# A fused attention and Fourier-mixing kernel: zero-tile dummy matmuls, half-wise table arguments, two-row folds and a new instruction order in the opening

## The chip, the cores and the metric

The kernel runs on one core of a Trainium2 chip. The metric is the device time of one execution in microseconds, as the median of several runs; less is better. The core has five engines with queues of their own: TensorE (PE in the profile, with its weight loads as PEld), VectorE (DVE), ScalarE (ACT), GpSimd (POOL) and SyncE (SP), which here only starts transfers.

## The reference

Cut to what matters. The inputs are x (8 batches, 8 heads, 512 rows, 64 columns), state (8, 8, 32, 64) and two weight matrices of 512 x 2048 and 2048 x 512, all in float32.

```python
scores = x @ state.T / sqrt(64);   a  = softmax(scores);   xread = a @ state
scores2 = state @ x.T / sqrt(64);  a2 = softmax(scores2);  sread = a2 @ x
z = concat([xread, sread], rows)              # per batch 544 rows x 512 columns (8 heads x 64)
mixed = real(fft(fft(z, rows), columns))
u = z + mixed
un = (u - mean(u)) / sqrt(var(u) + 1e-6)      # over the 512 columns
out = u + relu(un @ w_ch1) @ w_ch2
```

## The kernel before

The kernel works batch by batch. For each batch it makes the attention (scores, exponentials, two reads), folds the 544 rows and 512 columns by the symmetries of the Fourier transform, multiplies by cosine and sine tables along the rows (psum tiles `gp`) and along the columns (`yp`), adds the result to z (tile `U`), centres it (`ub`), transposes it (`tp`, `unT`), and runs the two layers: `ph` is a psum tile of the first layer, `hT` its result, `po` (batch 0) and `poA`, `poB` (later batches, in a Strassen form) those of the second. Weights live in `w1` and `w2` in bf16; eight transfers started by GpSimd bring and convert them, a quarter of a matrix each (`first_weights`, `second_weights`).

Nothing is scheduled by a compiler. Every operation is first recorded as a group (class `Recorder`, lines 21 to 64; `_Engine.__getattr__` makes the record), and `play` then issues the groups in the order of the list `ORDER`. So each engine's queue, and each transfer queue, follows that list. `BANKS` says which of six psum banks each tile gets. Consecutive matmuls into the same tile and bank form one group and cannot be separated. All operations have one line in the profile, L62, so they are told apart by their tiles.

Batch 0 has an opening of its own (`open_batch`, and the list from line 1261), because nothing else can run beside it:

- Loads. `load_x(0)` fills `xs` in seven pieces, four large (parts 0 to 3 of 128 rows; part 3 has 96 and three small pieces) and three small; `load_state(0, 1)` brings the state of batch 0 into `gen`. Two parts (2 and 0) go through ScalarE's queue, the others and the state through SP's.
- Tables. GpSimd makes integer ramps with iota (`pi_`, `gen`). `turn` makes from them the arguments of cosine and sine on VectorE, in four steps: counts, rests, products, ends. It makes two halves, [0] for the rows of x and [1] for the low rows (state rows and a few others). ScalarE turns them into the tables TC and TS; `minus` makes NC and NS, their negatives (tile NN). TEO is the table of the second axis.
- Attention. `cast_x` casts xs to bf16 (`xin`), `state_blocks` puts the state into a block form (`stb`), `turn_state` and `turn` transpose both on TensorE (tiles `warm` and `xTp`, copied to `sT` and `xT`), `score` multiplies them (`esp`), ScalarE takes exponentials (`EE`), `read` and `sread` form the reads (`xrp`, `warm`), and VectorE divides by the sums into XF, XR and XQ.
- Folds. `even(k)` and `odd(k)`, for k = 1 and 0, add and subtract reversed halves: Sm, then XE0 and XO0 (both in the memory of SS), and a column of ZB (in NN).
- Transform. `begin`, `low_of` (low rows, tables [1]) and `terms_of` (folds, tables [0]) accumulate four `gp` tiles; `out_of` copies them to G.
- Dummies. `warm(n)` records n matmuls of the identity tile `ident` with itself into a psum tile that nobody reads; `ORDER` spreads them over the opening (46 in all, 11 of them first).
- ScalarE loads a table of functions when it changes between exponentials and sines.

Batch 1 is loaded and cast meanwhile. GpSimd's `gate` operations make it wait for a chosen tile before it starts weight transfers: one on XO0, one on w1's last quarter, ahead of w2.

Of the kernel before, what the change touches and what calls it, by code (L numbers as in the profile page):

```python
# [20 lines left out]
class Recorder:  # L21
# [4 lines left out]
    def __init__(self, nc):  # L26
        self.nc, self.groups = nc, []
        for name in self.ENGINES:
            setattr(self, name, _Engine(self, name, getattr(nc, name)))
# [20 lines left out]
class _Engine:  # L50
# [3 lines left out]
    def __getattr__(self, what):  # L54
        f = getattr(self._engine, what)
        if not callable(f):
            return f

        def call(*args, **kw):
            out = kw.get("out", args[0] if args else None)  # L60
            key = (out.tensor.name, out.offset // 512 % 2) if self._name == "tensor" else None
            self._rec.add(self._name, lambda: f(*args, **kw), key)  # L62

        return call
# [3 lines left out]
        17 21 23 22 19 24 66 27-28 34 30 26 32 36 31 35 33 25 37 1 4 0 6 8 2 7 5 3 9 11 58 10 12 305 13-14 59 57 16 15 18 20 29  # L68
        42 40 39 38 41 86 89 43-46 49 48 47 51-52 50 53 55 54 80-82 96-97 87 90 56 98 109 111 93 113 112 110 83-85 94 114 124
        116 118 88 120 132 92 231 78 104 77 63 207 76 79 230 64 205 65 103 62 101 100 99 117 125 133 68 70 67 72-73 71 69 74 249  # L70
        75 95 115 134 136 135 137 146 153 147 91 122 138-139 154 140 155 108 141 229 144 206 142-143 201 106 149 126 148 150 128
        127 129 157 159 163 166 119 121 160-162 167 175 130 151 131 123 152 189 170 191 171-173 190 185 192 174 184 193 186
        197-199 158 169 165 156 178 180 168 216 179 164 182-183 196 194 187 209 188 212 176 181 195 177 211 217 214 210 213 107
        200 202-204 237 208 145 105 232 235 234 236 233 251 250 252 242 244 243 245 248 246-247 262 218 215 219 221 256 220
        223-226 253 222 227 260 259 255 254 257 261 258 271 273 451 272 274 315 263 269 277 275 270 278 281 283 267 265 328 264
        282 284 329 285 290-291 268 292-293 286 308 311-312 316 318 239 294 296-297 240 347 238 352 295 298-299 60 354 241 102
        320-321 313 309 314 310 322-323 371 279 306 330-331 326 317 287 319 266 327 307 402 372 332-333 453 334-336 338 454 337
        339 452 379 375-376 340 343 435 344 342 345 341 455 61 300 303 301 351 304 456 353 348-350 356 324 288 389 383 395 385
        369 387 393 406 391 403 399 397 390 325 289 276 521 396 280 386 384 388 394 370 392 400 398 418 404 410 448 381 411-412
        380 417 414 421-422 377 415 426 405 407-408 373 378 425 430-431 436 359-360 358 357 382 423 416 409 413 459 466 427 446  # L80
        428 419 447 432 429 420 508-509 437 433 504 457 434 401 438 302 506 510 458 505 346 507 363 362 365 367 364 361 366 473
        512 442 462 449 460 424 513 444 374 450 461 480 463 469 467 519 439 470 468 490-493 440 485 474 486 475 441 368 476 479
        702 477 483 478 489 482 487 484 514 488 528 522 464 515-516 560 552 530 494 499 497 531 536 544 517-518 523 532-533 503
        498 502 500-501 537-538 526 525 527 524 539-540 551 541 543 542 546-547 555 548 557 556 550 549 534 471 554 562 567 529
        465 481 561 545 535 520 553 568 472 582 607 563 571 569 565 495 564 572 570 566 576 591 598 558 496 583 592 608 577 579
        601 584 578 585 600 593 599 594 614 619 615 620 610 612 580 574 589 602 559 613 588 611 597 581 618 623 575 603 590
        644-645 681 634 666-667 687 691 646-647 631 586 630 670 629 228 628 648 658 657 659 587 660 663 662 661 511 604-605
        624-625 609 697 692 712 638 704-705 698 852 675 674 635 701 672 699 671 676 673 668 682 669 684 686 636 693-694 688 685
        683 706-707 639 708 713 709-710 721 716 720 724-725 717 719 718 632-633 606 643 726 627 695 748 742 794 714 722 732 727
        734 746 744 801 689 738 649 750 696 743 795 749 723 733 715 728 745 735 747 690 739 751 760 753 641 655 650 640 755 656  # L90
        642 637 652 736 740 803 729 758 664 810 767 653 651 756 754 757 665 730 711 731 677-678 779 792 772 761 802 737 804 759
        811 766 765 776 780 768 770 769 771 741 793 775 773 782 800 654 703 700 781 680 774 796 788 786 805 841 762 823 807 814
        812 822 763 813 806 787 626 783 789 797 817-818 849 834 816 832 837 904 838 819-820 842 833 851 595-596 821 752 826 621
        777 825 778 829 828 827 830-831 622 616 573 617 884 862 844 808 839-840 850 824 885 858-859 864 898 764 890 887 889 855
        853-854 809 1032 871-872 900 910 926 893 847 906 835 965 921 917 869 899 905 927 976 911 863 836 966 894 848 922 870 860
        843 861 865 873 846 845 867 874-878 868 901 895 879 896 916 880 907 918 897 883 882 881 908 914 923 1033 857 866 888 903
        856 892 891 886 977 919 912 937 915 924 909 920 913 938 978 933 928 942 970 939 983 952 954 988 1031 930 929 931 944 935
        943 934 932 971 936 984 940 955 941 990 1016 991 981 997 1007-1008 979 992 945-946 993 953 989 948 957 982 994 1000 798
        1001 1003-1004 1002 790 799 791 784 1005-1006 785 1009-1010 980 1017 1070 947 956 961 972 1210 1035 1034 1037 445 1064
        1069 1067-1068 1036 1012 967 1027-1028 985 1049 1076 1014 1166 1042 999 995 986 1013 1029-1030 996 1018 968 1021 1043  # L100
        1062 1038 1078 1024 1143 1096 1094 1040 1050 949 958 1077 1167 1063 1044 1019-1020 1045-1046 1048 1047 1056 1052 1025
        1011 1051 1054 1053 1071 1026 1073 1072 1060 1055 1041 1074 1088 1135 1084 1022 1123 1092 1098 1057 1090 1079 962 1015
        1144 1095 973 1039 1089 1097 1085 1136 1023 1124 1099 1075 1061 1058 1091 1093 1104 1161 1137 1118 1149 1080 1105-1107
        1081 1108 987 969 1066 1065 443 1109 1162 1150 1111-1112 1110 1209 925 950-951 355 959 1168-1169 1113 1102 1155 1086
        1194 1121 1159 1156 1087 1122 1160 1115 1138 1103 1101 1116 1119 1170 1114 1171 1120 1117 1173 1131 1126 1154 1127
        1211-1212 1059 998 1083 1130 1215 1125 1213-1214 1139 1145 1185 1175 1186 1190 1157 1218 1187-1188 1174 1158 1177 1204
        1191 1128 960 1172 974 1178 1180 1184 1179 1100 1183 1129 975 963-964 1205-1206 1151 1163 1265 1202 1207 1152 1219 1189
        1195 1234 1203 1208 1238 1198 1235 1200 1220-1221 1245 1182 1181 1197 1246 1222 1196 1164 1216 1251 1261 1227 1294 1273
        1249 1257 1267 1306 1240 1337 1192 1223 1199 1224 1226 1236 1225 1252 1242 1244 1262 1274 1229 1243 1230 1233 1231 1239
        1272 1291 1232 1201 1132 1140 1217 1266 1228 1250 1258 1146 1307 1295 1325 1338 1241 1268 1263 1255 1269 1289 1259 1270  # L110
        1264 1256 1260 1247 1284 1332 1320 1290 1248 1321 1333 1193 1328 1308 1365 1339-1340 1275 1287 1286 1285 1288 1309 1341
        1329 1342 1278 1276-1277 1279 1297 1302 1282 1298 1283 1237 1253 1165 1153 1316 1310 1296 1301 1343 1349 1351 1141-1142
        1350 1147 1354-1355 1133-1134 1148 1271 1353 1352 1299-1300 1322 1334 1356-1357 1346 1330 1292 1376-1377 1326 1314 1280
        1358 1366 1359 1370 1323 1335 1293 1303 1327 1281 1315 1331 1384-1385 1411 1421 1361 1371 1404 1391 1466 1380 1422 1412
        1405 1392 1381 1369 1368 1348 1378-1379 1386-1387 1398 1367 1388 1390 1389 1393 1406 1408 1394 1344-1345 1362 1375
# [53 lines left out]
def kernel(  # L169
# [30 lines left out]
    ctx.enter_context(tc.manual_schedule(engines={ET_.PE, ET_.DVE, ET_.Activation, ET_.Pool, ET_.SP}))  # L200


    ident = singles.tile([128, 128], BF16, name="ident")
    epst = singles.tile([128, 1], F32, name="epst")
    mhalf = singles.tile([128, 1], F32, name="mhalf")
    halfpi = singles.tile([128, 1], F32, name="halfpi")
# [1335 lines left out]
```

## Time and profile before

| what | us |
|---|---|
| runs (three) | 288.33, 288.52, 290.14; median 288.52 |
| profiled execution | 289.02 |
| its span, first to last instruction | 287.2 |
| TensorE busy | 275.9 (96%) |
| VectorE, ScalarE, GpSimd busy | 211.1, 161.7, 93.3 |
| first matmul | 4.32 |
| first matmul of the first layer (ph) | 23.43 |
| first matmul of the second layer (po) | 40.76 |
| granted TensorE clock (mean) | 0.995 |

All times inside the execution count from the start of the span; 1.8 us of the profiled execution lie outside of it. A line of the timeline gives start, busy time, engine, operation with its tiles and shapes, and in brackets the idle time before it with what ended it. A matmul's busy time includes the way through the array, so the distance between starts tells the rate. The granted clock of the profile's rows reads 1.00 from the start; whether TensorE runs at half or full rate is read from the distances of matmuls.

### The profile page before, as it was taken

What the parts mean: (1) busy time and instruction counts of PE and PEld (TensorE: products, weight loads), DVE (VectorE), ACT (ScalarE), POOL (GpSimd) and SP (SyncE); (2) the same over time, 40 slices, a digit from 0 to 9 for tenths busy, and PEclk for the clock granted to TensorE, in tenths of its full rate; (3) what the DMA queues carried; (4) which work ended last, traced back from release to release, by engine and by line L of the source; (5) the groups of instructions that cost most, each with busy time, mean ns of one, the idle gap of its engine ahead of it and who ended that gap; (6) DMA issues with size and microseconds to landing.
All of it is one profiled execution on the core that took longest, in us unless ns stands there. A gap on an engine that the chain in (4) does not pass through costs nothing.

```text
span 287.2 us, 6784 instructions
## 1 busy us (share of the span) xinstructions
PE 275.9 (96%) x2607; PEld 198.1 (69%) x2607; DVE 211.1 (74%) x557; ACT 161.7 (56%) x323; POOL 93.3 (32%) x227
## 2 busy tenths in 40 slices
PE   3999999999999999999999999999999999999992
PEld 2988985555655778566758777576577667687882
DVE  7688776468899988975798688959766578225882
ACT  5978584745936476368377564586566653254000
POOL 7673772570660043502812128006200028000000
PEclk9999999999999999999999999999999999999998
DMA  8999999966376237561398640313201520968466
GB/s 164 179 159 152 183 173 170 194 150 134 102 167 123 66 93 167 113 170 23 85 165 190 141 99 21 92 57 73 75 0 40 161 59 21 179 134 147 107 156 178
DMA packets 110972, 34.91 MB, mean 122 GB/s; under 512 B 101996, under 2 KB 106476, under 8 KB 110940
## 3 DMA queue, kind: packets, MB, share of 16 engines
q1 hardware_dynamic: 100220, 28.72, 48.5%
q0 software_dynamic: 4224, 4.19, 9.6%
q10 hardware_dynamic: 6496, 1.57, 2.5%
q8 instruction: 20, 0.33, 0.5%
q14 instruction: 12, 0.10, 0.1%
HBM read 22.41 MB, written 14.02 MB: 127 GB/s over the span
## 4 chain that ended last, share of the span: by engine, by line
PE 92%; DVE 4%; ACT 1%; issue 1%; POOL 0%; POOLq 0%
PE ph L62 41%; PE poA L62 18%; PE poB L62 13%; PE po L62 5%; PE gp L62 4%; PE yp L62 3%; PE esp L62 2%; PE xrp L62 1%; PE eTp L62 1%; PE xfp L62 1%; PE warm L62 1%; DVE gen L62 1%; DVE ot L62 1%; PE srp L62 1%; PE tp L62 1%
## 5 line engine op out<-in xcount | busy, mean ns | idle before, releaser
L62 PE MATMUL ph<-unT,w 128*128 128x512 bf16 (+2 forms) x768 | 129.6, 317 | 0.6 <-issue 0.5
L62 ACT ACTIVATE hT<-ph 128x512 bf16<-128x512 f32 x128 | 72.1, 596 | 77.6 <-PE ph L62 77.5
L62 PEld LDWEIGHTS <-w 128*128 128x128 bf16 x768 | 64.1, 98 | 42.9 <-issue 1.1
L62 PEld LDWEIGHTS <-hT 128*128 128x128 bf16 x632 | 60.5, 98 | 14.7 <-issue 0.3
L62 DVE SCALAR_TENSOR_TENSOR ot<-poA,rstd,U 128x256 f32<-128x256 f32 (+1 forms) x46 | 21.7, 475 | 16.5 <-PE poA L62 13.9
L62 POOL CAST xin<-xs 128x2048 bf16<-128x2048 f32 (+3 forms) x14 | 14.6, 1060 | 44.2 <-DMA xs<-in_x_dram 44.0
L62 PE MATMUL poB<-w,hT 128*128 128x256 bf16 x224 | 28.2, 273 | 0.0
L62 POOL TENSOR_TENSOR rstd<-rstd,mhalf 128x1 f32<-128x1 f32 x34 | 20.4, 608 | 1.1
L62 POOL TENSOR_TENSOR rstd<-mv,epst 128x1 f32<-128x1 f32 x14 | 2.5, 190 | 42.0 <-DVE mv L62 42.0
L62 ACT ACTIVATE ub<-U,S 128x512 bf16<-128x512 f32 (+1 forms) x22 | 15.1, 707 | 1.5 <-DVE U L62 1.3
L62 PE MATMUL po<-w,hT 128*128 128x512 bf16 x64 | 15.6, 379 | 0.0
L62 PE MATMUL poA<-TA,SB 128*128 128x256 bf16 x120 | 15.6, 273 | 0.0
L62 PE MATMUL poB<-TA,SA 128*128 128x256 bf16 x120 | 15.5, 272 | 0.0
L62 ACT CAST G<-gp 128x288 bf16<-128x288 f32 (+2 forms) x31 | 13.2, 481 | 4.0 <-PE gp L62 3.8
L62 DVE SCALAR_TENSOR_TENSOR U<-yp,XF 128x2 f32<-128x2 f32 (+1 forms) x24 | 10.0, 418 | 7.5 <-PE yp L62 5.3
L62 DVE SCALAR_TENSOR_TENSOR ot<-poB,rstd,ot 128x256 f32<-128x256 f32 x30 | 14.2, 477 | 1.0 <-PE poB L62 0.9
L62 PE MATMUL poA<-TC,hT 128*128 128x256 bf16 (+1 forms) x120 | 14.5, 265 | 0.1
L62 PE MATMUL poA<-w,hT 128*128 128x256 bf16 x112 | 14.5, 273 | 0.0
L62 ACT ACTIVATE junk<-U,S 128x512 bf16<-128x512 f32 x20 | 14.3, 716 | 0.2
L62 PE MATMUL poA<-TB,hT 128*128 128x256 bf16 x112 | 14.3, 272 | 0.0
L62 DVE SCALAR_TENSOR_TENSOR ot<-poB,rstd,U 128x256 f32<-128x256 f32 x15 | 7.2, 478 | 9.0 <-PE poB L62 9.0
L62 POOL COPY XT<-XR 32x514 bf16<-32x514 bf16 x7 | 4.2, 605 | 27.6 <-DVE U L62 16.5
(195 smaller groups left out, 475.6 us busy)
## 6 DMA issues: line engine op xcount, KB each, us to landing
xs<-in_x_dram SPq DMA_DIRECT2D x22, 256.0 KB, 3.9
w<-in_moe_w_ch_dram POOLq DMA_DIRECT2D x8, 512.0 KB, 6.6
out_dram<-ot SPq DMA_DIRECT2D x15, 256.0 KB, 2.4
r_dram<-ot SPq DMA_DIRECT2D x14, 256.0 KB, 2.3
out_dram<-r_dram SPq DMA_DIRECT2D x14, 256.0 KB, 3.7
xs<-in_x_dram SPq DMA_DIRECT2D x8, 192.0 KB, 3.7
xs<-in_x_dram ACTq DMA_DIRECT2D x2, 256.0 KB, 4.4
l_dram<-ot SPq DMA_DIRECT2D x2, 256.0 KB, 2.0
```

The source lines that it names most:

```text
L62: self._rec.add(self._name, lambda: f(*args, **kw), key)
```

## The change

1. A tile `blank` of zeros is set by VectorE at the start. `warm` multiplies it with itself, instead of `ident`. The first call records 48 dummies instead of 11. In the recorder, a matmul whose two operands are the same tile now is a group of its own, so the order can place each dummy by itself; 44 stand at the head of TensorE's queue, 83 are issued in all.
2. `turn` gives its four steps for each half. Half 0 is made at the start; `low_arguments` makes half 1 later. The sines and the negations are issued per half (288 wide instead of 576); those of half 1, and all negations, come after the exponentials of batch 0.
3. `even` and `odd` work on both rows k at once (1028 wide instead of 514, and so on).
4. The eight first loads form one group (`held`), issued in a fixed sequence. Within SP's queue part 1 now goes ahead of part 3. ScalarE casts three of four state blocks ahead of part 2 of x.
5. GpSimd makes the ramps of the x rows ahead of other constants.
6. `ORDER` and `BANKS` are new. What the new order does to the queues, read from the built programs:
   - VectorE casts part 0, copies the first transposed part, casts part 1, copies the state, casts part 3; half 1 of the arguments stands between the copies of xT and the reciprocals of batch 0.
   - GpSimd casts one part of x of batch 1, starts the first quarter of w1, does its part of XB, NN and stb, then starts the other three quarters of w1 together; after casts of batch 1 it starts w2's first quarter, after the copy of XR of batch 1 (XT) the second, after a root's first addition the last two. The gate on w1's last quarter now stands behind w2's transfers.
   - SP issues the loads of x of batch 1 in another order, and four pieces of x of batch 2 between the two transposes of the state of batch 2 that stood together before.
   - TensorE takes the sixteen steps of batch 0's first layer in another order; the quarter of w1 that arrives first is read first, and the last quarter is read from the tenth step on instead of the fifth. The first `gp` of batch 1 comes after fourteen steps instead of sixteen.
   - From about 44 us on, all engines' instructions stand in the same order in both kernels.

The diff, without the numbers of the order and the banks:

```diff
-            key = (out.tensor.name, out.offset // 512 % 2) if self._name == "tensor" else None
+            product = self._name == "tensor" and ("lhsT" not in kw or kw["lhsT"] is not kw["rhs"])
+            key = self._rec.held or ((out.tensor.name, out.offset // 512 % 2) if product else None)
...
+    blank = singles.tile([128, 128], BF16, name="blank")
+    nc.vector.memset(blank, 0.0)
...
-            for queue, n in ((nc.sync, None), (nc.scalar, 2), (nc.sync, 3), (nc.scalar, 0), (nc.sync, 4), (nc.sync, 5), (nc.sync, 6),
-                             (nc.sync, 1)):
+            nc.held = "first loads"
+            for queue, n in ((nc.scalar, 2), (nc.scalar, 0), (nc.sync, None), (nc.sync, 4), (nc.sync, 6), (nc.sync, 5), (nc.sync, 1),
+                             (nc.sync, 3)):
...
+            nc.held = None
...
-        def rests():
-            nc.vector.tensor_scalar(q2d, in0=q2d, scalar1=float(1 << 23), scalar2=-float(N), op0=ALU.subtract, op1=ALU.mult)
+        def rests(i):
+            nc.vector.tensor_scalar(q[:, i, :], in0=q[:, i, :], scalar1=float(1 << 23), scalar2=-float(N), op0=ALU.subtract, op1=ALU.mult)
...
+    def low_arguments():
+        nc.vector.tensor_copy(lo_, pi_[:, 2:3])
...
+        for step in turn_steps:
+            step(1)
...
-        nc.scalar.activation(TC, q1, AF.Sin, bias=halfpi, scale=-w_rows)
+    def sine_c(i):
+        nc.scalar.activation(TC[:, i], q1[:, i], AF.Sin, bias=halfpi, scale=-w_rows)
...
-        def even(k):
-            nc.vector.tensor_add(Sm[:, k], XF[:, k], XR[:, k])
+        def even():
+            nc.vector.tensor_add(Sm, XF, XR)
...
-            nc.tensor.matmul(warmed["tile"][:, 0:128], lhsT=ident, rhs=ident, start=True, stop=True)
+            nc.tensor.matmul(warmed["tile"][:, 0:128], lhsT=blank, rhs=blank, start=True, stop=True)
...
-    turn_products()
-    turn_ends()
-    sine_s()
-    sine_c()
+    sine_s(0)
+    sine_c(0)
     exp_again()
-    warm(11)
+    warm(48)
...
     exp2()
+    low_arguments()
...
-    minus(NC, TC)
-    minus(NS, TS)
+    minus(NC[:, 0], TC[:, 0])
+    minus(NS[:, 0], TS[:, 0])
     sin_table()
+    sine_s(1)
+    sine_c(1)
...
-    even(1)
+    even()
     second_sines()
     second_halves()
+    minus(NC[:, 1], TC[:, 1])
+    minus(NS[:, 1], TS[:, 1])
...
-    odd(1)
+    odd()
     terms_of(2, 1), terms_of(3, 1)
-    even(0)
...
-    odd(0)
```

## The prediction

> **What bounds the kernel now.** I read the chain of waits first. It gives TensorE nearly everything, so a change pays only if TensorE's main stream starts sooner.
>
> ```profile
> PE 92%; DVE 4%; ACT 1%; issue 1%; POOL 0%; POOLq 0%
> ```
>
> Then TensorE's waits, longest first. After its first instruction it is starved for about 1.5 us in the whole span; the one long wait is at the start, where the dummies wait for the identity tile that GpSimd makes.
>
> ```profile
> PE warm L62 <- POOL ident L62: 4.3, 1, 4.3
> PE tp L62 <- ACT ub L62: 0.5, 1, 0.5
> PE ph L62 <- issue: 0.5, 1, 0.5
> ```
>
> "Never starved" is not "full speed". The timeline of TensorE (start, busy us, operation) shows what the busy share hides:
>
> ```profile
> 4.32 1.35 PE L62 MATMUL warm<-ident 128*128 128x128 bf16 x11 [4.32 <-POOL ident L62]
> 8.32 0.58 PE L62 MATMUL esp<-xT,sT 128*128 128x128 bf16 x4
> ...
> 9.99 0.61 PE L62 MATMUL esp<-xT,sT 128*128 128x128 bf16 x4
> ...
> 11.71 0.83 PE L62 MATMUL warm<-ident 128*128 128x128 bf16 x12
> ...
> 17.98 0.23 PE L62 MATMUL gp<-NN,SS 128*128 128x144 bf16 x1
> ...
> 22.45 0.40 PE L62 MATMUL tp<-ident,ub 128*128 128x128 bf16 x4 [0.50 <-ACT ub L62]
> ...
> 23.43 1.05 PE L62 MATMUL ph<-unT,w 128*128 128x128 bf16 x16
> ```
>
> The 11 dummies start 107 ns apart; the 12 at 11.71 start 56 ns apart. The trace's clock record has the step to full rate at 11.5 us, 7.2 us after the first matmul. So all score matmuls of batch 0 (esp, from 8.32) run at half rate. From 23.43 the layers of the network (ph, po, poA, poB) fill TensorE to the end. The question is: how much earlier than 23.43 can that stream begin? VectorE's and ScalarE's timelines give the other links:
>
> ```profile
> 6.45 0.49 DVE L62 TENSOR_SCALAR gen<-gen 128x576 int32<-128x576 int32 x1
> 6.86 0.74 DVE L62 CAST xin<-xs 128x512 bf16<-128x512 f32 x2
> ...
> 12.99 0.70 DVE L62 TENSOR_TENSOR XR<-xrp,rs 128x512 bf16<-128x512 f32 x1
> ...
> 16.49 0.75 DVE L62 TENSOR_TENSOR Sm<-XF,XR 128x514 bf16<-128x514 bf16 x2
> ```
>
> ```profile
> 10.86 1.65 ACT L62 ACTIVATE EE<-esp 128x512 bf16<-128x512 f32 x3 [0.58 <-PE esp L62]
> 12.40 0.68 ACT L62 ACTIVATE NN<-TC 128x576 bf16<-128x576 bf16 x1
> ...
> 20.30 1.28 ACT L62 ACT_TABLE_LOAD   x1
> ```
>
> VectorE casts the inputs only after both halves of the table arguments (6.86). From 12.99 to 18.9 it is nearly full. ScalarE's exponentials wait for half-rate scores, and its table load at 20.30 stands ahead of the copy and centring that TensorE awaits at 22.45.
>
> **The change, part by part.** The queues after the change are known from the built program; the times below are my estimates from rows of this trace.
>
> *Zero tile and dummies.* The tile `blank` is VectorE's second instruction (about 0.07 us, done near 1.45), so dummies start at 1.5, not 4.32. Forty-four stand ahead of the first real transposes; in all 83 instead of 46. At 107 ns the 44 last 4.7 us, to 6.2. The real transposes wait behind them: the part cast by ScalarE is ready at 4.9. Before, those transposes began at 6.48, so this is free only while the clock rises.
> When does it rise? By the row of before, 7.2 us after the first matmul: at 8.7. [...] By the row the whole sum below loses 0.6.
>
> *Table arguments per half.* Two counts (0.45 each), a 576-wide rest (0.98), two products (0.51) and a 576-wide absolute (0.49) stand before the casts. Afterwards only half 0 and one count do: 0.40 + 0.50 + 0.50 + 0.27 + 0.40 = 2.1 us from about 3.95. First cast 6.1 instead of 6.86. The rest of half 1 (0.50 + 0.50 + 0.27) goes between the xT copies and the first reciprocals, 9.2 to 11.0, where VectorE idled 1.22 and 0.97 for scores.
> ScalarE: two 576-wide sines, 6.45 to 7.82, become two 288-wide ones (estimate 0.45 each, from the 32x288 row of 0.53 less overlap), 5.8 to 6.65; the exponential's table is loaded at 7.9 instead of 9.1. The other two sines and four 288-wide negations (1.7 us, against 1.25 for two wide ones) come after the exponentials. ScalarE gains 0.8 us of work in all, hidden while its exponentials end early.
>
> *Loads.* The eight first loads keep their bytes and queues; only the last two of SP change places, and the state's blocks are cast ahead of x. The landings in the trace were 2.8 for the state, then 4.2, 5.7, 6.9 and 7.9 for the four parts of x; the last stays 7.9, so this is worth nothing by itself. It is the floor: the last cast cannot start before 7.95.
>
> *The sum to the first product.* With the clock up near 7: first scores 8.0 (8.32 before), the four exponentials 8.6 to 11.05 (9.23 to 12.4), first XR at VectorE at 11.3 instead of 12.99: **-1.7**. VectorE's chain from there (four 0.70 products, reciprocals, XB and XQ copies) keeps its 3.2 to 3.5 us.
>
> *Folds two rows wide.* Before: from 16.49 to the G copy at 18.93, 2.44 us in fourteen instructions. After: 0.68 + 2 x 0.22 + 2 x 0.07 + 2 x 0.35 + 0.06, about 2.0 us in eight. But the first product needs Sm of both rows now, and TensorE's part-1 terms start about 1.1 us into the folds, or when ScalarE's negations are done (estimate 15.4) and six matmuls have used them. So terms start near 16.1 instead of 17.98: **-1.8**, no more from the folds, because the negations are next.
>
> *ScalarE's tail.* Negations, TEO and the low sine end at 17.6; the first G copy, due at 17.1, is 0.5 late, but the last G is due only at 18.3. Table load 18.55 instead of 20.30, centred block at 20.4, so tp at 20.5 to 20.7: **-1.8**.
>
> *Order anew: queues.* GpSimd casts one part of x of batch 1 before its first weight load; that load's data lands near 10.3 (estimate, by bytes), so the load issues near 11.2, as before (11.32). The other three of w1 issue together near 14 to 16.4 instead of 16.1, 16.9 and 21.4, and the last quarter is first read by the tenth layer step instead of the fifth. That removes the 5.8 us in which GpSimd waited at `gate` for w1. The first two of w2 come at about 20 and 28 (31.3 and 36.2 before). The last two wait behind a root that needs VectorE's mean and variance, and issue near 37.1 and 38.3 (38.98 and 40.38). On SP the loads of batch 2 move ahead of the second state transpose and start some 4 us earlier, beside w1's last quarter, which has slack. From about 44 us on every engine's order is the same as before, so the lead is carried to the end.
>
> Sum: 289.02 (profiled execution: span 287.2 and 1.8 around it) - 1.8 = 287.2. That execution was 0.5 above the median of the runs, 288.52; against the median, 286.7. I take **286.7**.
>
> **The rivals.**
> 1. *The clock rises late* (slower side). [...] The transposes wait to 6.2, first scores 8.66 instead of 8.32, XR near 13.45 instead of 12.99, and ScalarE, now with sines and negations behind the last exponential (13.3), ends its table load at 22.2 instead of 21.6. That is +0.6: **289.1**. It decides once the step comes after about 11; every further us of half rate costs up to 0.5. [...] Against: 4.7 us without a gap is longer than any such stretch before 8.3 in the old trace.
> 2. *The lead is given back at a load.* w2's last quarter landed at 48.8 and was first read then, with no slack. If it again takes 8.5 us from issue (38.3), it lands at 46.8, exactly when needed; with batch 2's loads and transposes beside it, 1 us late. Gain 0.8: **287.7**. Against: two quarters of w2 are out of the way long before.
> 3. *More than summed.* VectorE's small instructions at the start, and the ScalarE chain, are estimated with care; if the step comes near 5 and the negations finish sooner, 3 us: **285.4**. Against: the last x part at 7.95 is a floor.
> 4. *A smaller gain.* The clock steps up at 8.7, as the row of before says, and ScalarE is 0.5 slower than summed: 0.7, **287.8**.
>
> **How the numbers follow.** Forecast 0.52, rival 1 0.17, rival 2 0.10, rival 3 0.12, rival 4 0.09. The forecast's own range, 286.2 to 287.4, comes from a step between 5 and 8.7. The range for 8 in 10 takes in rivals 2 and 4 and most of 1 and 3: 285.1 to 289.0. A measurement of this kernel tells about 1% from no change, 2.9 us: under 285.6 or over 291.4. Faster gets rival 3 and a little of the forecast's edge, 0.14; slower needs rival 1 with the clock down to 15 or an unseen stall, 0.08; within 1% 0.78.
>
> **What would show it.** Dummies from about 1.5; 56 ns spacing from about 7 (rival 1: after 11); first XR near 11.3; first gp on SS near 16.1; the table load ahead of the first centred block near 18.6; first ph near 21.6; then no idle time between 21.6 and 55 (rival 2: a po waiting for w2 near 46). I am wrong if the first ph comes at 23 or later, or if it comes at 21.6 and the end has not moved.

## The result, and the profile after

The changed kernel takes **287.88 us** (median of 19 runs, 287.44 to 288.44; a twentieth, at a granted clock of 0.756 over the whole execution, took 362.66 and is left out of every comparison). The kernel before took 288.92 beside it (20 runs, 287.72 to 290.71). The ratio is 0.9958, 95% interval 0.9942 to 0.9974: some 1.0 to 1.2 us, about six tenths of the 1.8 that the prediction summed, and well within 1% of no change. The spread has shrunk as well, from 3.0 us to 1.0 us.

The profiled execution took 287.47 us, its span 285.7 (before: 289.02 and 287.2). The chain of waits, then TensorE's waits (total, times, longest), of the changed kernel:

```profile
PE 87%; DVE 7%; DMA 2%; issue 1%; ACT 1%; SPq 1%; DVEq 0%
```

```profile
PE warm L63 <- DVE blank L63: 1.5, 1, 1.5
PE xTp L63 <- DVE xin L63: 1.4, 3, 0.9
PE tp L63 <- DVE U L63: 0.4, 1, 0.4
PE xfp L63 <- DVE XR L63: 0.2, 1, 0.2
```

TensorE's 4.3 us wait for the identity tile is gone, and waits for VectorE have come up: for the casts of x (xTp), and two small ones, xfp for XR and tp for U, which the kernel before did not have. The timeline of TensorE, changed kernel:

```profile
1.53 3.91 PE L63 MATMUL warm<-blank 128*128 128x128 bf16 x44 [1.53 <-DVE blank L63]
5.28 0.39 PE L63 MATMUL xTp<-ident,xin 128*128 128x128 bf16 x4
...
8.19 0.38 PE L63 MATMUL esp<-xT,sT 128*128 128x128 bf16 x4
...
16.93 0.23 PE L63 MATMUL gp<-NN,SS 128*128 128x144 bf16 x1
...
21.48 0.40 PE L63 MATMUL tp<-ident,ub 128*128 128x128 bf16 x4
...
22.39 1.05 PE L63 MATMUL ph<-unT,w 128*128 128x128 bf16 x16
...
28.40 0.40 PE L63 MATMUL xfp<-stb,ET 128*128 128x260 bf16 x2 [0.21 <-DVE XR L63]
...
50.45 0.38 PE L63 MATMUL tp<-ident,ub 128*128 128x128 bf16 x4 [0.39 <-DVE U L63]
```

Forty-four dummies in 3.9 us cannot all have started 107 ns apart (that would take 4.7): the trace's clock record steps to full rate at 4.25, in the middle of them, and from there on they start 56 ns apart. Every score matmul now runs at full rate (four in 0.38 us instead of 0.58). The first ph comes 1.04 us earlier than before (22.39, 23.43). VectorE and ScalarE of the changed kernel:

```profile
6.00 0.41 DVE L63 CAST xin<-xs 128x512 bf16<-128x512 f32 x1
...
7.32 0.43 DVE L63 CAST xin<-xs 128x512 bf16<-128x512 f32 x1 [0.58 <-DMA xs<-in_x_dram]
...
8.46 0.43 DVE L63 CAST xin<-xs 128x512 bf16<-128x512 f32 x1 [0.38 <-DMA xs<-in_x_dram]
...
10.95 0.85 DVE L63 TENSOR_SCALAR gen<-gen 128x288 int32<-128x288 int32 x1
...
12.09 0.70 DVE L63 TENSOR_TENSOR XR<-xrp,rs 128x512 bf16<-128x512 f32 x1
...
15.48 0.69 DVE L63 TENSOR_TENSOR Sm<-XF,XR 128x1028 bf16<-128x1028 bf16 x1 [0.31 <-ACT XR L63]
```

```profile
9.81 1.75 ACT L63 ACTIVATE EE<-esp 128x512 bf16<-128x512 f32 x3 [0.48 <-PE esp L63]
...
14.84 0.60 ACT L63 CAST XR<-warm 32x512 bf16<-32x512 f32 x1 [0.67 <-POOL XB L63]
...
19.53 1.28 ACT L63 ACT_TABLE_LOAD   x1
```

The casts no longer wait for arguments but for data (0.58 and 0.38), and the last exponentials wait for the scores of that data. GpSimd's XB, for which ScalarE waits at 14.84, stood behind a cast of batch 1's state, which landed at 14.28 (GpSimd):

```profile
14.34 0.28 POOL L63 CAST stb<-gen 32x128 bf16<-32x128 f32 x1 [0.60 <-DMA gen<-in_state_dram]
```

To see where the lead goes, the two traces are laid over each other: by TensorE's tiles up to the first ph, and from 48 us on by VectorE's instructions, counted from the end (its records line up one to one that far back). Before minus after: 1.0 us from the first product on SS to the first ph; 0.5 at 48 us, 0.45 from 61 us to 176; 1.08 from there to the last `ot`. So **0.6 us of the lead is lost between 22 and 61 us, and 0.63 us is won at 174 us**, where only the trace of before has a stall:

```profile
173.86 1.04 PE L62 MATMUL poB<-w,hT 128*128 128x256 bf16 x8
175.36 1.02 PE L62 MATMUL ph<-unT,w 128*128 128x512 bf16 x4 [0.47 <-issue]
```

No dependency is shown for it ("issue").

### The profile page after: what moved, and what is told of

Read it like the earlier page. It is cut to its first block, busy times and chain, and to the rows that moved or that the text cites. A ratio compares the mean times of both kernels' runs of the same rounds, so it can differ in the third digit from the quotient of the medians.

```text
span 285.7 us, 6835 instructions
## 1 busy us (share of the span) xinstructions
PE 275.2 (96%) x2615; PEld 199.0 (70%) x2644; DVE 210.6 (74%) x554; ACT 162.0 (57%) x327; POOL 92.5 (32%) x227
## 3 DMA queue, kind: packets, MB, share of 16 engines
q10 hardware_dynamic: 6496, 1.57, 2.6%
## 4 chain that ended last, share of the span: by engine, by line
PE 87%; DVE 7%; DMA 2%; issue 1%; ACT 1%; SPq 1%; DVEq 0%
PE ph L63 39%; PE poA L63 18%; PE poB L63 13%; PE gp L63 4%; PE po L63 3%; PE yp L63 2%; DVE U L63 2%; DMA xs<-in_x_dram 2%; PE esp L63 2%; PE eTp L63 1%; PE xrp L63 1%; DVE XR L63 1%; PE xfp L63 1%; DVE ot L63 1%; SPq L63 1%
## 5 line engine op out<-in xcount | busy, mean ns | idle before, releaser
L63 PE MATMUL ph<-unT,w 128*128 128x512 bf16 (+2 forms) x743 | 127.9, 315 | 1.4
```

## The experiments

e1 and e11 try the dummies in the old order, e2 the change without the early ones; e3, e5, e6 and e7 take the other parts one at a time; e12 takes away the waits for input; e4 and e10 look for the place where the lead was lost; e8 and e9 are the two kernels once more.

One table first. "Step" is the clock record's step to full rate, "last ot" the end of VectorE's last store tile; after it the transfers out and the end of the program took 4.3 to 4.9 us in every trace, whichever the kernel, so last ot tells kernels apart better than the span of one trace. "Before" beside the first four runs was 288.68 us (29 runs), beside the next four 288.96 (20), beside the last four 288.74 (29).

| kernel | median (range) us | ratio to before, 95% | step | first XR | first ph | last ot |
|---|---|---|---|---|---|---|
| before | 288.92 (287.72-290.71) | 1 | 11.54 | 12.99 | 23.43 | 282.45 |
| changed | 287.88 (287.44-288.44) | 0.9958 (0.9942-0.9974) | 4.25 | 12.09 | 22.39 | 281.36 |
| e1 before + early zeros | 287.06 (286.82-288.87) | 0.9955 (0.9941-0.9969) | 5.49 | 11.97 | 22.40 | 280.86 |
| e2 changed, late start | 287.82 (287.34-289.45) | 0.9979 (0.9959-0.9999) | 7.50 | 11.94 | 22.58 | 281.56 |
| e3 changed, state load early | 287.64 (287.17-287.94) | 0.9967 (0.9952-0.9982) | 5.15 | 12.13 | 22.37 | 281.40 |
| e4 changed, ones early | 287.03 (286.71-289.04) | 0.9959 (0.9935-0.9983) | 4.63 | 12.27 | 22.53 | 280.96 |
| e5 changed, absolute later | 287.71 (287.28-288.47) | 0.9961 (0.9947-0.9974) | 4.29 | 11.94 | 22.49 | 281.47 |
| e6 changed, arguments first | 287.65 (287.61-288.40) | 0.9965 (0.9951-0.9978) | 4.18 | 12.02 | 22.36 | 281.34 |
| e7 changed, folds by row | 287.84 (287.42-288.99) | 0.9967 (0.9955-0.9980) | 4.99 | 11.85 | 22.23 | 281.38 |
| e8 changed again | 287.64 (287.38-288.32) | 0.9961 (0.9947-0.9975) | 5.09 | 12.05 | 22.50 | 281.48 |
| e9 before again (one run) | 287.95 | | 10.19 | 12.42 | 22.86 | 281.24 |
| e10 changed, gaps filled | 287.25 (286.50-288.15) | 0.9956 (0.9937-0.9975) | 7.34 | 12.28 | 22.72 | 281.08 |
| e11 before + 12 early zeros | 288.63 (287.77-289.55) | 1.0003 (0.9982-1.0023) | 9.42 | 12.07 | 22.49 | 282.35 |
| e12 changed, no last landings | 287.39 (287.07-287.95) | 0.9957 (0.9940-0.9974) | 5.01 | 10.65 | 22.00 | 280.98 |

### e1: the early dummies alone

```diff
     ident = singles.tile([128, 128], BF16, name="ident")
+    blank = singles.tile([128, 128], BF16, name="blank")
+    tc.nc.vector.memset(blank, 0.0)
...
-            nc.tensor.matmul(warmed["tile"][:, 0:128], lhsT=ident, rhs=ident, start=True, stop=True)
+            nc.tensor.matmul(warmed["tile"][:, 0:128], lhsT=blank, rhs=blank, start=True, stop=True)
...
-    warm(11)
+    warm(44)
```

> The kernel before, with one thing of the change: a zero tile set by VectorE's first instruction, all dummies multiply it, and 44 instead of 11 stand first on TensorE. Theory A (the early clock is the gain): dummies from about 1.1 us, full rate from 4 to 5 us instead of 11.5, scores at 56 ns a matmul, first XR near 12.2 instead of 12.99, the time near 287.9 (-1.0), and its runs within about 1 us of each other instead of 3. Theory B (the gain is the shorter work of VectorE and ScalarE: arguments per half, folds, order): first XR and the time move by less than 0.3 us (288.6 or more), since ScalarE's two wide sines and the casts behind the wide arguments still hold the exponentials.

Theory A holds, and by more than the -1.0 expected: -1.6 us in the median (-1.3 by the ratio, whose interval is -0.9 to -1.7), and eleven of the twelve runs lie within 0.4 us of each other (286.82 to 287.22). The old kernel's TensorE with the early dummies:

```profile
0.98 4.76 PE L62 MATMUL warm<-blank 128*128 128x128 bf16 x44 [0.98 <-DVE blank L205]
...
21.42 0.40 PE L62 MATMUL tp<-ident,ub 128*128 128x128 bf16 x4 [0.49 <-ACT ub L62]
...
22.40 1.05 PE L62 MATMUL ph<-unT,w 128*128 128x128 bf16 x16
```

The first ph is at 22.40, the changed kernel's at 22.39. So **one part of the change alone brings the whole lead at the first ph**, and by the end the old order with it is 0.5 us ahead of the changed kernel (last ot 280.86 against 281.36 and 281.48). By the two intervals the medians of e1 and of the change cannot be told apart. Beside e1, though, ran e3, which is the changed kernel but for the place of one load: 287.64, its runs from 287.17 to 287.94, that is 0.6 us above e1, as the two traces say.

### e2: the change without the early dummies

```diff
         for n in order:
+            if 75 <= n < 108:
+                continue
...
-            nc.tensor.matmul(warmed["tile"][:, 0:128], lhsT=blank, rhs=blank, start=True, stop=True)
+            nc.tensor.matmul(warmed["tile"][:, 0:128], lhsT=ident, rhs=ident, start=True, stop=True)
```

> The changed kernel without the early dummies: 33 of the 44 at TensorE's head are left out and all dummies multiply the identity tile, so that TensorE begins when GpSimd has made it. Arguments per half, folds and order stay. Theory A: the clock steps up near 11 us as before, the score matmuls run at 107 ns, XR comes about 1 us later, the time goes back to 288.7 to 289.0 and its runs spread over 2 to 3 us. Theory B: the time stays at 287.9 to 288.2, since the rest of the change is still there.

Neither is decided. The median, 287.82, is just under theory B's 287.9 to 288.2; the spread, 2.1 us, is theory A's (before: 3.0, changed: 1.0). The trace says why the theories did not part: the changed order makes the identity tile earlier (first matmul at 3.89 instead of 4.32) and keeps other dummies between the transposes, and in the profiled execution the clock stepped at 7.50, before the first scores at 8.32. So the late clock, which was to be brought back, was not there. e1 shows that the early dummies are enough in the old order; that the changed order needs them is not shown.

### e3, e5, e6, e7: the other parts, one at a time

```diff
 e3 (ORDER; 58 is the load of batch 1's state)
-  19 62 66 61 9-10          ...  185 193 59-60 58 67
+  19 62 66 61 58 9-10       ...  185 193 59-60 67
 e5 (152 is the absolute value that ends half 1's arguments; 198 a reciprocal, 199 the first XR)
-  182 152 190 198-199 191
+  182 190 198-199 152 191
 e6 (149-152 are half 1's counts, rest, product, absolute)
-  148 43-45 149 18 24       ...  222 132 150-151 182 152 190
+  148 43-45 149-152 18 24   ...  222 132 182 190
 e7
-            nc.vector.tensor_add(Sm, XF, XR)
-            nc.vector.tensor_add(XE0[:, :, 128:256], Sm[:, :, 256:128:-1], Sm[:, :, 256:384])
...
+            for k in (1, 0):
+                nc.vector.tensor_add(Sm[:, k], XF[:, k], XR[:, k])
+                nc.vector.tensor_add(XE0[:, k, 128:256], Sm[:, k, 256:128:-1], Sm[:, k, 256:384])
...
```

> The changed kernel with the load of batch 1's state issued two places earlier on SP, ahead of the first two parts of x of batch 1 that stand before it now. It landed at 14.28 us, and GpSimd, ScalarE and VectorE waited in turn behind it (0.60, 0.67, 0.31 us). Theory C (this load is a link of the chain): it lands near 12.5, the three waits go, ScalarE's table load and the first ph come 0.3 to 0.6 us earlier, and the end moves by as much (287.4). Rival D (the chain has another link beside it, or later stages give it back): first ph moves by less than 0.15 or the end by less than 0.2.

Rival D. GpSimd's cast of the state began at 13.73 without a wait, and VectorE's wait went too, but ScalarE then waited for TensorE at the same place (0.45 instead of 0.67), and the first ph stood at 22.37. ScalarE and GpSimd of e3:

```profile
14.66 0.60 ACT L63 CAST XR<-warm 32x512 bf16<-32x512 f32 x1 [0.45 <-PE warm L63]
```

```profile
13.73 0.28 POOL L63 CAST stb<-gen 32x128 bf16<-32x128 f32 x1
```

> The changed kernel with one VectorE instruction moved: the absolute value that ends half 1's arguments comes after the first XR product instead of between the reciprocals ahead of it. In the changed kernel's trace it stood there from 10.95 and took 0.85 us (0.31 for half 0), and the first XR began at 12.09 though its score product was ready near 11.6. Theory G (the second half of the arguments sits on the chain to the first XR): first XR near 11.6 (-0.45), first ph 0.2 to 0.45 earlier, the time 0.2 to 0.4 below the changed kernel's. Rival H (the next link, the state rows or TensorE's products on XB, is as late): XR moves, first ph by less than 0.1 and the time not at all.

Rival H. VectorE of e5:

```profile
11.53 0.31 DVE L63 RECIPROCAL rs<-esp 128x8 f32<-128x8 f32 x2 [0.32 <-PE esp L63]
11.94 0.70 DVE L63 TENSOR_TENSOR XR<-xrp,rs 128x512 bf16<-128x512 f32 x1
12.55 0.30 DVE L63 TENSOR_SCALAR gen<-gen 128x288 int32<-128x288 int32 x1
12.77 0.68 DVE L63 TENSOR_TENSOR XF<-xrp,rs 128x512 bf16<-128x512 f32 x1
...
13.56 0.29 DVE L63 TENSOR_TENSOR XQ<-warm,rcs 128x128 bf16<-128x128 f32 x1
```

The reciprocals now wait for TensorE's sums of the exponentials, XR gains 0.15 instead of 0.45, and XQ, for which TensorE waits, comes no earlier (13.56; 13.49 in the changed kernel). First ph and time are the changed kernel's.

> The changed kernel with the split of the table arguments undone on VectorE: all of half 1 (rest, product, absolute; 1.3 us) comes before the casts again, the sines stay split. The prediction counts on the split: first cast 1.3 us later (7.3), exponentials 0.3 to 0.5 us later, first XR and end later by 0.3 to 0.5 us. Theory G: half 1 leaves the stretch before the first XR, where it stood on the chain, and the casts wait for the landings at 7.3 and 8.34 anyway; XR at 11.8 to 12.1, the end the same as the changed kernel's within 0.15 or up to 0.3 earlier. That is, the split is worth nothing.

Theory G. With the split undone on VectorE the first cast moves from 6.00 to 7.36, and yet (VectorE, then ScalarE, of e6):

```profile
7.36 0.42 DVE L63 CAST xin<-xs 128x512 bf16<-128x512 f32 x1
...
12.02 0.70 DVE L63 TENSOR_TENSOR XR<-xrp,rs 128x512 bf16<-128x512 f32 x1
```

```profile
9.42 2.39 ACT L63 ACTIVATE EE<-esp 128x512 bf16<-128x512 f32 x4
```

The four exponentials start 0.7 us later but run back to back, because their data has landed meanwhile; they end at 11.81 instead of 11.56. First ph 22.36, time 287.65. **On VectorE the split of the arguments is worth nothing.** The sines stayed split; what that is worth alone was not tried.

> The changed kernel with the folds of batch 0 one row at a time again (fourteen VectorE instructions, row 1 first) in the same place of the order. Folds take 2.44 us instead of 2.0. Theory I (TensorE's products on XB set the start of the products on the folded rows, near 16.9 in the kernel before with the early clock and in the changed kernel alike): first product on SS at 16.9, first ph within 0.1, the time the same as the changed kernel's within 0.15. Rival J (the folds are the link): the last folds end 0.45 us later, first ph and the end 0.3 to 0.45 later.

Theory I. The first product on SS comes at 16.69, the first ph at 22.23, 0.2 us earlier if anything (this execution's first scores were at 8.03, 8.22 in e8); the time, 287.84, is e8's within the runs' spread. **Folds two rows wide are worth nothing** either. From XQ's transposes at 13.98 TensorE is busy almost without a break, with products on XB, until it takes SS at 16.93, and that stream, not the folds, is last.

> The changed kernel unaltered, on the same chip as the three runs beside it, as their reference and as a second trace. Every theory: clock step between 4 and 6 us, first ph near 22.4, TensorE's gap at tp of 0.6 us near 50, no stall of TensorE near 174 us, the time 0.3 to 0.5% under the kernel before, runs within about 1 us.

As expected: step at 5.09, first ph at 22.50, the gap at tp (0.615 us from one start to the next), no stall near 174.

### e9: the kernel before, once more

> The kernel before, unaltered: one more trace of it. Two things are read there. The clock's step: theory K (it falls in a free phase) has it anywhere from 3.4 to 7.5 us after the first matmul at 4.3, so 7.7 to 11.8; rival L (it always needs the 7.2 us of the first trace) has it at 11.5 again. And TensorE's stall of 0.74 us near 174: if it is a property of the old order it is there again; if it comes and goes with the execution it may be absent, as in every other trace so far. The time between 287.6 and 290.5.

Theory K: the step was at 10.19, 5.9 us after the first matmul, not 7.2. The lower edge of its range, 3.4 us, was not shown: this opening gave 5.9 and 7.2 alone. And the stall near 174 is absent:

```profile
173.21 1.04 PE L62 MATMUL poB<-w,hT 128*128 128x256 bf16 x8
174.08 1.03 PE L62 MATMUL ph<-unT,w 128*128 128x512 bf16 x4
```

It is in one of the two traces of the old kernel and in none of the twelve others. The 0.63 us that the change seemed to win there belong to that execution. What caused it stays open.

### e11: how many dummies

Against e1:

```diff
-    warm(44)
+    warm(12)
```

> The kernel before with the zero tile, but 12 dummies at TensorE's head instead of 44: about 1.3 us of matmuls from 1.0 us, then little until the transposes near 5.3. Theory A as the prediction has it (the clock wants a stretch of matmuls without a gap): the 12 lift nothing, the step comes between 8 and 11.5, the time near 288.3 to 288.7 with runs spread over 2 us. Rival M (any early start of TensorE is enough, length does not matter): step near 5.5 as with 44, the time 287.1 and the runs within 1 us.

Theory A: with twelve the step came at 9.42 (5.49 with 44), and the ratio is 1.0003. Whether the number of dummies or the gap behind them made the difference was not tried. The first three lines are the opening in e11, the last two its later waits:

```profile
0.98 1.46 PE L62 MATMUL warm<-blank 128*128 128x128 bf16 x12 [0.98 <-DVE blank L205]
6.12 0.82 PE L62 MATMUL warm<-ident,stb 128*128 128x128 bf16 x4 [3.68 <-ACT stb L62]
6.73 1.64 PE L62 MATMUL xTp<-ident,xin 128*128 128x128 bf16 x12
...
29.49 1.07 PE L62 MATMUL ph<-unT,w 128*128 128x128 bf16 x16 [0.64 <-DMA w<-in_moe_w_ch_dram]
...
43.88 1.02 PE L62 MATMUL po<-w,hT 128*128 128x512 bf16 x4 [0.66 <-DMA w<-in_moe_w_ch_dram]
```

But this execution was not slow for the reason expected. Its step came at 9.42 and cost 0.1 us at the first ph (22.49; 22.40 in e1); 1.4 us more were lost later, 1.3 of them in two waits for weights. With the old order w1's last quarter is issued at 20.4 to 21.4 and needed about 6.2 us after the first ph. It landed 7.4 us after its issue in e1, 0.8 us before it was needed; 8.15 and 8.35 us in the two traces of before, 0.1 us ahead of the need and 0.1 us behind it; and 9.0 us here, 0.7 us too late. GpSimd, which waits for it at `gate`, then issued w2 late. With the changed order that quarter landed at 26.1 and its first reader comes later. So the new order removes a loss that the old one has in some executions. How the 1.57 us between the medians of e11 and e1 divide into clock and loads, one trace cannot say.

The four traces of the old order give the price of the clock, with the step and the first ph: 5.49 and 22.40, 9.42 and 22.49, 10.19 and 22.86, 11.54 and 23.43. A step as late as 9.42 costs 0.1 us at most against one at 5.49; the likely reason is that the scores from 8.3 on wait for data anyway. Each us after it costs (23.43 - 22.49) / (11.54 - 9.42) = 0.44 us.

This price does not reach the medians. Even the latest step seen, 11.54, cost 1.0 us at the first ph, and the other trace of before (10.19) 0.5, while e1's runs are 1.3 to 1.6 us under those of before. So the dummies are the cause, but only a part of what they save is shown to be the clock; where the rest is lost stays open. The traces name the weight loads, which in the old order come with no slack, as a candidate.

### e12: the floor

```diff
-    for i in (0, 3, 1):
-        cast_x(0, nc.vector.tensor_copy, i, i + 1)
+    x_landed = xs_of[0].rearrange("p (i c) -> p i c", i=4)
+    for i in (0, 3, 1):
+        nc.vector.tensor_copy(xin_bufs[0][:, i:i + 1, 1:513], x_landed[:, 0:1])
```

> The changed kernel with the two last inputs to VectorE's casts of batch 0 taken from a part of x that has landed before (part 0, at 6.0 us) instead of parts 1 and 3 (7.3 and 8.3): the computation is of other data for these rows, the work is the same. Theory N (the landings of x are the floor under the first XR, which the prediction put at 11.3): last cast near 7.2 instead of 8.46, the four exponentials back to back, first XR near 11.2, first ph 0.5 to 0.8 earlier and the end with it (287.0). Rival O (another link, VectorE's or ScalarE's queue or the table load, is within 0.3 us of the landings): XR moves by less than 0.4 and the end by less than 0.3.

Theory N for XR, less than it for the end. VectorE, then TensorE, of e12:

```profile
7.33 0.41 DVE L63 CAST xin<-xs 128x512 bf16<-128x512 f32 x1
...
10.65 0.70 DVE L63 TENSOR_TENSOR XR<-xrp,rs 128x512 bf16<-128x512 f32 x1
...
15.09 0.70 DVE L63 TENSOR_TENSOR Sm<-XF,XR 128x1028 bf16<-128x1028 bf16 x1 [0.88 <-ACT XR L63]
```

```profile
14.51 0.30 PE L63 MATMUL gp<-TS,XB 128*128 128x288 bf16 x1 [0.57 <-POOL XB L63]
...
22.00 1.05 PE L63 MATMUL ph<-unT,w 128*128 128x128 bf16 x16
```

Without the waits for the last two landings XR comes 1.4 us earlier: they are the floor. Of these 1.4 us only 0.4 to 0.5 reach the first ph (and about 0.25 the median, 287.39 against e8's 287.64 in another session), because the next link stands close behind: XB, which GpSimd makes behind the cast of batch 1's state, and that waits for its load. GpSimd of e12:

```profile
13.95 0.28 POOL L63 CAST stb<-gen 32x128 bf16<-32x128 f32 x1 [0.85 <-DMA gen<-in_state_dram]
```

It is the wait that e3 took away, to no effect: there TensorE, behind the landings of x, was as late. **Two links lie side by side; either one removed alone shows little.** What both removed together would show was not tried.

### e4 and e10: where the lead was lost between 22 and 61 us

```diff
 e4 (ORDER; 443 and 445-450 are seven memsets of ones into stb, 375 GpSimd's clearing of the same tile)
-  419 375 426 ... 451 481 445-446 449 482 450 487 484 491 442 492 447 485 ... 475 477-478 443 448 495
+  419 375 445-450 443 426 ... 451 481 482 487 484 491 442 492 485 ... 475 477-478 495
 e10 (e4, and 378, the 32 matmuls of srp)
-  353 378 351 ... 358 382 381
+  353 351 ... 358 378 382 381
```

> The changed kernel with the seven memsets of ones (stb) set ahead of batch 1's first U addition on VectorE, in its wait of 2.8 us for yp. In the changed kernel's trace three of them and the waits between stand in the U chain, which is 0.37 us longer than before, and TensorE's gap at tp is 0.61 instead of 0.25 us. Theory E (the memsets cost the lead there): the tp gap falls to about 0.25 and the end by 0.3 (287.5). Rival F: the gap falls but a later wait takes it back, or the gap has another cause; the end moves by less than 0.1.

Theory E. The stretch of VectorE at batch 1's sums, changed kernel first, e4 after it:

```profile
44.00 0.69 DVE L63 TENSOR_TENSOR U<-yp,XF 128x510 f32<-128x510 f32 x1 [2.81 <-PE yp L63]
44.78 0.27 DVE L63 MEMSET stb<- 32x12 bf16 x3
45.09 0.16 DVE L63 TENSOR_TENSOR U<-yp,XF 128x2 f32<-128x2 f32 x1
45.35 0.07 DVE L63 MEMSET stb<- 32x12 bf16 x1
45.45 0.69 DVE L63 TENSOR_TENSOR U<-yp,XR 128x512 f32<-128x512 f32 x1
```

```profile
42.88 0.68 DVE L63 MEMSET stb<- 32x12 bf16 x7 [1.55 <-POOL stb L63]
44.14 0.89 DVE L63 TENSOR_TENSOR U<-yp,XF 128x510 f32<-128x510 f32 x2 [0.59 <-PE yp L63]
44.94 0.68 DVE L63 TENSOR_TENSOR U<-yp,XR 128x512 f32<-128x512 f32 x1
```

TensorE of e4, where the twelve matmuls of tp now are one row (the changed kernel's last four waited 0.39 at 50.45):

```profile
49.59 0.83 PE L63 MATMUL tp<-ident,ub 128*128 128x128 bf16 x12
```

Seven memsets that take 0.68 us in an idle stretch had cost TensorE 0.55 us among the twelve matmuls of tp (from the first start to the last 1.17 us in e8, 0.62 in e4), and from there the whole rest: first ph is as in e8 (22.53 and 22.50), last ot 0.52 us earlier (280.96 and 281.48), the median 287.03. That is e1's time (287.06, run beside it): without the loss at the memsets, the rest of the change adds to the dummies nothing that the runs show.

> The changed kernel with the seven memsets of ones ahead of the U chain, as in the run before on them alone, and with the 32 matmuls of srp moved behind the next ph block, into the gap of 0.21 us in which TensorE waits at xfp for XR (as the kernel before has them). Theory E: both losses of the lead between 22 and 51 us go; first ph stays near 22.4, the lead over the unaltered changed kernel is 0.2 at 43 us and 0.6 from 51 us to the end, so 287.0, below the kernel before with the early clock alone. Rival F: ET is read sooner than it is ready once srp is away from the eTp transposes, the gap reappears there, and no more than the 0.4 of the memsets is won.

Rival F. Counted from the first ph, xfp came 0.18 us earlier (5.84 instead of 6.02) and stayed so for some 4 us; then TensorE, at 32.87, paused 0.18 us in a row of ph for a reason that the profile doesn't show, and at yp nothing of it was left (20.98 in both). What e10 wins over e8 from the first ph on, 0.6 us, is the memsets'. Its median, 287.25, is not better than e4's. No version was found that beats e1 and e4 by more than the runs' spread.

## Why the prediction was right and where it was wrong

**The direction and the main cause, the early dummies, were right, the sum too large.** The forecast of 286.7 is 1.2 us too low: -1.8 was summed, -1.0 was measured between the medians. The measured 287.88 lies outside the forecast's own range (286.2 to 287.4) and inside the wide one that took in the rivals.

*Zero tile and dummies: right.* Dummies from 1.53, as said, and the step between 4.18 and 7.34 in nine traces of the changed order with 44 dummies and in e1 (the forecast: near 7). No run on which the sum could rest shows its step near 7, nor the 5 at which its range begins: both were the author's estimate, and what the runs showed in their place is these 4.18 to 7.34. The row of the old trace, a step 7.2 us after the first matmul, did not repeat: the same opening had 5.9 in e9, and with the 44 dummies first the delays were 2.65 to 5.81. The clock records show a grid: the stretch at full rate is 273.07, 276.48 or 279.89 us long in all fourteen traces, which is 80, 81 and 82 times 3.413, so its begin and its end lie a whole number of 3.41 us apart, while the place of the step differs from execution to execution. What must stand ahead of the step is shown only in part. The 3.41 us before it held 2.6 us of dummies in e6 and 2.7 in the changed kernel's trace; in e10 2.4 us of dummies stood before 3.93, which is 3.41 us ahead of its step at 7.34, and no step came there. In e11 the 3.41 us before the step (6.01 to 9.42) held 3.3 us of matmuls, all but 0.9 of them transposes; in the trace of before the stretch from 4.71 to 8.13 held 3.0 us, 2.0 of them transposes, and no step came at its end, though after 2.6 us of dummies one came in e6. Whether transposes do as much for the clock as dummies is not shown.

*The sum to the first product: the step that failed.* It put XR at 11.3, -1.7; the trace has 12.09, -0.9. The exponentials were summed to 8.6 to 11.05, as if scores were always ready; measured, 8.73 to 11.56, because the last three wait for x landing at 7.30 and 8.34 (with the old order the last part landed at 7.9 to 8.2 in four traces, with the new one at 8.1 to 8.65 in ten, and XR follows it: 8.11 and 11.85 in e7, 8.65 and 12.28 in e10). The prediction named the landing at 7.95 as a floor, and then used it only against a larger gain, not in its own sum. e12 shows the floor at its true height, 1.4 us of XR; e6 shows that VectorE's casts, which the sum made earlier, were not what the exponentials needed.

*Arguments per half: the times right, the worth wrong.* First cast 6.00 (said: 6.1), the exponential's table loaded at 7.6; worth nothing on VectorE (e6), because the data comes later than either. *Folds: 2.0 us, exactly as summed, worth nothing* (e7): behind them stands TensorE's stream on XB, not the negations, so SS came at 16.93 instead of 16.1. *ScalarE's tail*: the table load at 19.53 (said: 18.55) ended at 20.81, when U was just done, so it held up tp by 0.1 us at most; VectorE's half of ub starts at nearly the same time as ScalarE's (20.83 and 20.93). *Loads*: said to be worth nothing by themselves; no run tried them alone.

*"The lead is carried to the end": wrong.* The prediction compared queues from 44 us on and found them equal. That holds from 48 us on only. The seven memsets of ones straddled the line: three had stood at 38.4 and were moved, behind GpSimd's later clearing of the tile, to 44.8, into the chain of U additions (e4, which moves all seven: 0.55 us). With the wait at xfp the lead shrank by 0.6 us. "No idle time between 21.6 and 55" was the sign to look for, and it failed as said it would.

*The base.* The -1.8 was taken from one execution of before. It had the latest clock step of the two seen (11.54, worth 0.57 us at the first ph over the other's 10.19), and a stall of 0.63 at 174. The second trace of before ends its work at 281.24, no later than the changed kernel.

*The rivals.* The clock did not rise late (1). No po waited for w2 in the changed kernel (2), although its last two quarters were issued at 39.2 and 40.3 (said: 37.1 and 38.3), no earlier than before; just this loss was seen in the old order, in e11. The number of rival 4, 287.8, is the measured one, but for another reason than it gave: the clock was early and its gain was used up by the landings and the memsets.

## What to carry to other kernels

Where an opening waits for data, put a stretch of work on zeros before the first real matmul so that the clock is up when the data comes (here 44 matmuls without a gap did it, with the step at 4.18 to 7.34; with 12 it came at 9.42), and then ask which landing is last before pricing any shorter instruction queue. Read the lead at several places, not only where the change is: a few memsets, three of them 0.27 us together, moved into the one chain that TensorE waits for, cost 0.55 us, while the folds and VectorE's split arguments brought nothing. And take the base from more than one execution where the clock's step decides part of it (11.54 and 10.19 in the two of before).

## What the runs showed of the hardware that was not expected

- The clock's step after TensorE's first matmul varied between 2.65 us (e6) and 5.81 (e10) for the same 44 gap-free dummies, between 5.9 and 7.2 for the old opening, and the stretch at full rate that it begins was 273.07, 276.48 or 279.89 us long, 3.41 apart. Zeros times zeros were enough: the step came at 4.25 in the changed kernel and at 5.49 in e1, with nothing else on TensorE before it.
- VectorE's 288-wide absolute took 0.85 us at 10.95, while GpSimd cast x from 10.74 to 11.39, and 0.30 when e5 moved it to 12.55, with no such cast beside it. Five traces have the cast beside it (0.85 to 0.88), four have not (0.30 to 0.31).
- A weight quarter started by GpSimd landed 7.4 to 9.0 us after its issue in four executions of the same order, enough to decide whether TensorE waits.
